# A decode kernel's last weight row in two halves, with a branch hint, a load and a copy moved

## The chip, the cores and the metric

The kernel runs on one core of one Trainium2 chip. The metric is the device time of one execution, in microseconds. Each timed run also gives the **span** of the profile, from the core's first counted instruction to its last; the execution time is about 1.25 us longer than the span in the kernel before.

## The reference, cut to what matters

One token goes through two blocks, whose results are added: attention over a cache of 65,536 positions (32 query heads on 4 cached heads), and a small network of layers with w1 to w4.

```python
xn = _layernorm(x)
return x + _A_ref(xn, k_cache, v_cache, wq, wo) + _B_ref(xn, w1, w2, w3, w4)
# _A_ref: q = xn @ wq; softmax(q k^T / sqrt(128)) v for each head; @ wo
# _B_ref: ... h2 = gelu(layernorm(x1) @ w3) @ w4;  w4 is 3584 x 1024
```

The caches are 134 MB, all inputs 170 MB, the output is 1024 numbers of two bytes. Every input is read once. So the kernel is a stream of loads with work beside it, and a short tail after the last byte.

## The kernel before

All large loads go through SyncE's queue into three slots of on-chip memory: wq, w1, w2, w3, then K and V blocks in turn, then wo, and last w4 in four transfers of 17, 7, 3 and 1 "rows". Such a row is what one step of the contraction needs: 1024 columns on each of 128 partitions, 2 KB a partition. TensorE's program runs the four cached heads in a loop; the instructions before and after the loop are straight code.

The tail, cut to what the change touches:

```python
w4_parts = [(0, 17), (17, 7), (24, 3), (27, 1)]
...
def out_rows(items, reads, last=False):          # [1,256] products in 4 column groups
    for lhs, rhs in items:
        for jj in range(4):
            ... e.matmul(S_ps[32*jj:32*jj+1, 0, 0:256], lhs, rhs[:, 256*jj:256*jj+256], ...)
...
def wo_rows():
    ...
    _op(q_dve, lambda e: e.tensor_copy(pT_f[0:1, 0, :], S_ps[0:1, 1, :]), ...)
    _op(q_act, lambda e: e.activation(pT_f[32:33, 0, :], S_ps[32:33, 1, :], ACTF.Copy), ...)
...
for i, (r0, nr) in enumerate(w4_parts):
    out_rows(...)                                # waits for transfer i
_op(q_dve, lambda e: e.tensor_copy(orow[:, :], OUT), ...)
ev_out = _dma(q_sp, chan("out"), lambda e: e.dma_start(out=out..., in_=orow[0:97:32, :]), ...)
```

The products of w4 start inside TensorE's tail, behind a hint. The hint belongs to a dummy branch at the end that is never taken, whose target is the tail itself:

```python
nc.br(name + "_b", engines=[e]);  label(name + "_b")
hint = eng.mark_branch_hint_location()           # the hint instruction stands here
q.emit(eng, q.ops[at:])                          # the products of w4
eng.br_eq(one, 1, on_true=name + "_end", on_false=name + "_t")
label(name + "_t");  eng.nop(nofuse=True)
eng.br_eq(one, 0, on_true=name + "_b", on_false=name + "_end").branch_hint(hint)
```

## Time and profile before

| | kernel before |
|---|---|
| execution time, median of 3 runs | 400.37 us |
| span of the profiled run | 399.0 us |
| VectorE busy, TensorE busy | 55%, 44% |
| bytes read from HBM, mean rate | 169.87 MB, 426 GB/s |
| last transfer of w4 lands | 396.47 us |

The busy lines of a page are averages over stages and say little here; the line of DMA slices, full from end to end, says nearly everything. The prediction shows it with the lines of the tail. Two more lines of the page, from its list of DMA queues (packets, MB, share of the 16 engines' time):

```profile
q8 instruction: 4, 0.07, 0.1%
q14 instruction: 3, 0.02, 0.0%
```

The page calls them "instruction": they are not data but the engines' own code, and it counts their time on the same 16 DMA engines. Inside the span stand four packets of 16 KB, 1.02 to 1.11 us each, and three of 8 KB, 0.32 us each.

### The profile page before, as it was taken

The page shows a single profiled execution, that of the slowest core. Times are in us where ns is not written, and L with a number is a line of the kernel's source. Part 1 is how long each engine was busy: PE and PEld are TensorE (multiplying, and loading weights), DVE is VectorE, ACT ScalarE, POOL GpSimd, SP SyncE. Part 2 cuts the span into 40 slices and gives each one's busy share as a digit, 9 for nine tenths or more (in the row PEclk, how much of TensorE's full clock was granted, in tenths as well). Part 3 has the DMA queues.
Part 4 walks back from the last instruction along what each step waited for, and adds up shares of the span by engine and source line. Part 5 has one row for each costly group of instructions (what it writes and reads, how often), then busy time and mean ns, then how long its engine had stood idle before and what let it go on. Part 6 is the DMA issues. An engine that isn't in the chain of part 4 may idle for free.

```text
span 399.0 us, 3448 instructions
## 1 busy us (share of the span) xinstructions
PE 176.1 (44%) x1539; PEld 58.8 (15%) x1484; DVE 221.3 (55%) x260; ACT 23.9 (6%) x50; POOL 7.6 (2%) x31
## 2 busy tenths in 40 slices
PE   0034768148034713570357036413651462147394
PEld 0011334012001200120012001101120110012232
DVE  0024221995298549843984597269647952896200
ACT  1000000011001100110011002001100110011000
POOL 5000000000000000000000000000000000000000
PEclk9998656556755765565557555855585558555979
DMA  9999899999999999999999999999999999999995
GB/s 421 421 386 494 383 428 480 447 416 427 421 420 435 420 466 453 421 427 421 420 440 420 453 460 427 421 421 420 434 434 440 473 427 421 420 421 427 431 410 233
DMA packets 3759, 169.97 MB, mean 426 GB/s; under 512 B 548, under 2 KB 552, under 8 KB 808
## 3 DMA queue, kind: packets, MB, share of 16 engines
q1 hardware_dynamic: 3608, 169.87, 98.8%
q8 instruction: 4, 0.07, 0.1%
q10 hardware_dynamic: 144, 0.00, 0.0%
q14 instruction: 3, 0.02, 0.0%
HBM read 169.87 MB, written 0.00 MB: 426 GB/s over the span
## 4 chain that ended last, share of the span: by engine, by line
DMA 58%; DVE 25%; PE 13%; issue 1%; ACT 1%; SPq 1%; POOL 0%
DMA KV<-in_A_k_cache_dram 45%; DVE KV L460 18%; DMA KV<-in_B_w_dram 8%; DMA KV<-in_A_x_dram 6%; PE S_ps L411 3%; PE OT_ps L518 2%; DVE mrow L481 2%; PE M_ps L426 2%; PE S_ps L474 2%; PE S_ps L379 2%; ACT p_sb L496 1%; DVE Yall L395 1%; DVE pT_f L509 1%; PE PT_ps L505 1%; DVE pT_f L419 1%
## 5 line engine op out<-in xcount | busy, mean ns | idle before, releaser
L460 DVE STREAM_TRANSPOSE KV<-KV 128x4096 f32<-128x4096 f32 x32 | 140.3, 4421 | 43.3 <-DMA KV<-in_A_k_cache_dram 43.3
L474 PE MATMUL S_ps<-KV,Ycur 128*32 128x512 bf16 x512 | 60.7, 623 | 127.2 <-DVE KV L460 127.2
L518 PE MATMUL OT_ps<-KV,pT_f 128*32 128x512 bf16 x512 | 46.2, 500 | 1.2 <-DVE pT_f L509 1.2
L474 PEld LDWEIGHTS S_ps<-KV,Ycur 128*32 128x32 bf16 x512 | 14.3, 126 | 159.0 <-DVE KV L460 141.4
L496 ACT ACTIVATE p_sb<-S_ps,brun 128x1024 bf16<-128x1024 f32 x16 | 17.8, 1113 | 275.0 <-DVE brun L494 174.5
L509 DVE STREAM_TRANSPOSE pT_f<-PT_ps 128x512 f32<-128x512 f32 x32 | 22.5, 702 | 14.0 <-PE PT_ps L505 14.0
L481 DVE TENSOR_REDUCE mrow<-S_ps 128x1 f32<-128x1024 f32 x16 | 19.3, 1206 | 11.3 <-PE S_ps L474 11.3
L484 PE MATMUL M_ps<-Rm,Lmat 128*128 128x16 bf16 x16 | 3.1, 194 | 38.1 <-DVE Rm L482 38.1
L505 PE MATMUL PT_ps<-p_sb,permR 128*128 128x512 bf16 x32 | 18.4, 576 | 0.8
L529 DVE SCALAR_TENSOR_TENSOR O_acc<-O_acc,ff,OT_ps 128x512 f32<-128x512 f32 x12 | 9.0, 748 | 13.9 <-PE OT_ps L518 13.9
L518 PEld LDWEIGHTS OT_ps<-KV,pT_f 128*32 128x32 bf16 x512 | 12.9, 114 | 23.6 <-issue 15.5
L411 PE MATMUL S_ps<-KV 128*32 128x512 bf16 x88 | 12.6, 565 | 2.7 <-DVE KV L359 2.7
L339 DVE CAST KV<-KV 128x8 f32<-128x8 bf16 x1 | 0.2, 171 | 22.1 <-DMA KV<-in_A_x_dram 22.1
L578 PE MATMUL S_ps<-KV,o_bf 128*1 128x512 bf16 x64 | 9.4, 466 | 5.0 <-DMA KV<-in_A_wo_dram 5.0
L426 PE MATMUL M_ps<-ident_f,pT_f 64*128 64x2 f32 (+2 forms) x32 | 7.9, 372 | 2.5 <-DVE pT_f L419 2.5
L484 PEld LDWEIGHTS M_ps<-Rm,Lmat 128*128 128x128 bf16 x16 | 1.7, 104 | 49.3 <-DVE Rm L482 49.3
L582 DVE COPY pT_f<-S_ps 1x512 f32<-1x512 f32 x1 | 0.7, 679 | 14.4 <-PE S_ps L578 14.4
L426 PEld LDWEIGHTS M_ps<-ident_f,pT_f 64*128 64x128 f32 (+2 forms) x32 | 7.7, 326 | 5.0 <-DVE pT_f L419 3.4
L419 DVE COPY pT_f<-S_ps 64x512 f32<-64x512 f32 (+1 forms) x3 | 2.1, 685 | 11.3 <-PE S_ps L411 11.3
L364 PE MATMUL M_ps<-KV 8*128 8x8 bf16 x1 | 0.2, 181 | 16.0 <-DVE Dmat_f L363 16.0
L505 PEld LDWEIGHTS PT_ps<-p_sb,permR 128*128 128x128 bf16 x32 | 3.3, 103 | 26.7 <-ACT p_sb L496 14.7
L379 PE MATMUL S_ps<-KV 128*32 128x512 bf16 x64 | 6.2, 571 | 1.4 <-DVE KV L359 1.4
(88 smaller groups left out, 85.6 us busy)
## 6 DMA issues: line engine op xcount, KB each, us to landing
KV<-in_B_w_dram SPq DMA_DIRECT2D x1, 7168.0 KB, 48.2
KV<-in_B_w_dram SPq DMA_DIRECT2D x1, 4352.0 KB, 27.4
KV<-in_B_w_dram SPq DMA_DIRECT2D x2, 2048.0 KB, 28.2
KV<-in_B_w_dram SPq DMA_DIRECT2D x1, 1792.0 KB, 31.4
KV<-in_B_w_dram SPq DMA_DIRECT2D x1, 768.0 KB, 32.7
KV<-in_B_w_dram SPq DMA_DIRECT2D x1, 256.0 KB, 32.9
KV<-in_A_k_cache_dram SPq DMA_DIRECT2D x8, 46.6
KV<-in_A_v_cache_dram SPq DMA_DIRECT2D x8, 27.9
```

What stands on the lines that cost most here:

```text
L379: fns.append(lambda e, j=j, b=b, jj=jj: e.matmul(S_ps[32 * jj:32 * jj + 32, b, :], xn_bf[:, j:j + 1].broadcast_to([P, 32]), KV[:, 0, j * H ...
L411: fns.append(lambda e, j=j, k=k, mv=mv: e.matmul(S_ps[32 * (k % 4):32 * (k % 4) + 32, bank + k // 4, :], vec[:, j:j + 1].broadcast_to([P, ...
L426: fns.append(lambda e, b=b, nb=nb, c=c: e.matmul(M_ps[:, c0 + 16 * b + c:c0 + 16 * b + 4 * nb:4], pT_f[0:32 * nb, b, c:512:4], ident_f[0:3 ...
L460: _op(q_dve, lambda e: e.transpose(out=KV32[:, s, o:o + 4096], in_=KV32[:, s, o:o + 4096]), reads=[b_KV[s][sub]], writes=[b_KV[s][sub]], l ...
L474: fns.append(lambda e, we=we, cm=cm, mv=mv: e.matmul(S_ps[32 * cm:32 * cm + 32, n % 4, :], Ycur[:, we, :, :].rearrange("p a g -> p (a g)") ...
L481: _op(q_dve, lambda e: e.reduce_max(mrow[:, k:k + 1], S_ps[:, 2 * k:2 * k + 2, :].rearrange("p b c -> p (b c)"), axis=AX.X), reads=b_S[2 * ...
L496: _op(q_act, lambda e: e.activation(p_sb[:, :, :].rearrange("p b c -> p (b c)"), S_ps[:, 2 * k:2 * k + 2, :].rearrange("p b c -> p (b c)") ...
L505: _op(q_pe, lambda e: e.matmul(PT_ps[:, :], permR[:, :], p_sb[:, n % 2, :], start=True, stop=True), reads=[b_p[n % 2], b_const], writes=[b ...
L509: _op(q_dve, lambda e: e.transpose(out=pT_f[:, n % 2, :], in_=PT_ps[:, :]), reads=[b_PT], writes=[b_pT[n % 2]], loop=True)
L518: fns.append(lambda e, q=q, q4=q4: e.matmul(OT_ps[32 * q4:32 * q4 + 32, g % 2, :], pT_bf[:, n % 2, q, :, 1], KV[:, s, 8192 * sub + 512 * q ...
L529: _op(q_dve, lambda e: e.scalar_tensor_tensor(out=O_acc[:, 0:512], in0=O_acc[:, 0:512], scalar=ff[:, k:k + 1], in1=OT_ps[:, k, :], op0=ALU ...
L578: _grp(q_pe, [lambda e, j=j, jj=jj: e.matmul(S_ps[32 * jj:32 * jj + 1, 1, :], o_bf[:, j:j + 1], KV[:, 0, j * D + 512 * jj:j * D + 512 * (j ...
```

## The change

The change wants a shorter tail. The last w4 row comes in two transfers of 512 columns. The first 24 rows are summed in one bank (of PSUM, the memory that TensorE writes its sums to) and copied to on-chip memory while the rest is under way; rows 24 to 26 are multiplied in 128-column pieces into one bank for each half; and each half of the output has its own last products, its own addition and its own store, the first from ScalarE, the second from SyncE. The second half reuses the weights that the first half has loaded. The order of the output's columns in the banks is changed to fit, in the products of wo too (not shown). Three small edits come with it: the tail's dummy branch goes, and the hint stands for the loop's own closing branch; x is loaded by SyncE, after wq, instead of by ScalarE; the second row of wo's sums is copied by VectorE.

```diff
-        _dma(q_act, chan("x"), ... x_bf ...)
         kv_load(0, "s0", rows_src(A_wq, 0, 8), 8 * HQD)
+        _dma(q_sp, chan("x"), ... x_bf ...)
...
-            _op(q_act, lambda e: e.activation(pT_f[32:33, 0, :], S_ps[32:33, 1, :], ACTF.Copy), ...)
+            _op(q_dve, lambda e: e.tensor_copy(pT_f[32:33, 0, :], S_ps[32:33, 1, :]), ...)
...
-        w4_parts = [(0, 17), (17, 7), (24, 3), (27, 1)]
+        w4_parts = [(0, 17 * D), (17 * D, 24 * D), (24 * D, 27 * D), (27 * D, 27 * D + 512), (27 * D + 512, 28 * D)]
...
-        for i, (r0, nr) in enumerate(w4_parts):
-            out_rows(...)
-        _op(q_dve, lambda e: e.tensor_copy(orow[:, :], OUT), ...)
-        ev_out = _dma(q_sp, chan("out"), ...)
+        for i in range(n_bulk):                   # n_bulk = 2
+            out_rows(i)
+        _op(q_dve, lambda e: e.tensor_copy(ost, S_ps[:, 0, 0:256]), ...)
+        for r in range(24, 27):
+            out_halves(r, (0, 1), 2, first=(r == 24))
+        for hf, q_out in ((0, q_act), (1, q_sp)):
+            out_halves(27, (hf,), 3 + hf, last=True)
+            _op(q_dve, lambda e, hf=hf: e.tensor_tensor(out=orow[:, 128*hf:128*hf+128], in0=ost[...], in1=S_ps[:, 2 + hf, 0:128], op=ALU.add), ...)
+            ev_out.append(_dma(q_out, chan("out%d" % hf), ... 512 outputs ...))
...
+        loop_br = [... the last branch of TensorE so far, which closes the loop ...][-1]
         q_pe.emit(nc.tensor, q_pe.ops[marks[-1]:pe_cut])
-        hinted_tail(nc.tensor, q_pe, pe_cut, "pe")
+        bass.BassInstruction(loop_br).branch_hint(nc.tensor.mark_branch_hint_location())
+        q_pe.emit(nc.tensor, q_pe.ops[pe_cut:])
```

## The prediction

> **What bounds the kernel now.** I read the page from the top: busy shares first, then the slices, then the chain, then the stretches in which the change lies. VectorE, the busiest engine, is busy for 55% of the span, TensorE for 44%. The slices show what is full:
>
> ```profile
> DMA  9999899999999999999999999999999999999995
> GB/s 421 421 386 494 383 428 480 447 416 427 421 420 435 420 466 453 421 427 421 420 440 420 453 460 427 421 421 420 434 434 440 473 427 421 420 421 427 431 410 233
> ...
> HBM read 169.87 MB, written 0.00 MB: 426 GB/s over the span
> ```
>
> The 16 DMA engines are busy from the first slice to the last, which falls to a half. 169.87 MB at about 430 GB/s are 395 us, so all but some 4 us of the 399.0 us are the transfer of inputs, and the change moves as many bytes. Time can only come out of the two ends, or be lost as a hole in the stream. I look for holes in SyncE's waits:
>
> ```profile
> SPq L290 <- PE OT_ps L518: 255.5, 7, 38.8
> ```
>
> SyncE waits to reuse the one V slot; this wait is long, but the page gives 27.9 us from issue to landing of a V load. One load is 8.39 MB, 19.5 us at 430 GB/s, so about 8 us of other transfers still lie ahead of it when it is issued. A delay of TensorE or VectorE under 8 us never reaches the end. The last stretch, from the timeline:
>
> ```profile
> 395.86 0.50 PE L566 MATMUL S_ps<-KV,gh_bf 128*1 128x256 bf16 x12 [0.92 <-DMA KV<-in_B_w_dram]
> ...
> 396.51 0.28 PE L566 MATMUL S_ps<-KV,gh_bf 128*1 128x256 bf16 x4 [0.16 <-DMA KV<-in_B_w_dram]
> 396.85 0.42 DVE L648 CAST orow<-S_ps 128x256 bf16<-128x256 f32 x1 [7.29 <-PE S_ps L566]
> 397.30 0.62 SPq L649 DMA_DIRECT2D out_dram<-orow  x1
> ```
>
> The last w4 row lands at 396.47. Then come its four products, the cast, the store's issue, and (SyncE's waits) 1.0 us until the store has landed. This exposed tail is 399.0 - 396.47 = 2.5 us, 0.6% of the span: the change's direct prize is a part of that.
>
> A second reading: the last row does not land at once. Windows of the last microseconds:
>
> ```profile
> 394.00:395.00 1.00, 0.93 (x28) 0.57 (x28) 0.00 (x0) 0.00 (x0) 0.00 (x0) 1.00 0.50 186
> 395.00:396.00 1.00, 0.14 (x8) 0.14 (x12) 0.00 (x0) 0.00 (x0) 0.00 (x0) 1.00 0.25 96
> ```
>
> The last two columns are the DMA share and GB/s: half the engines' time is used from 394 to 395, a quarter from 395 to 396. The trace's sixteen semaphore steps of the last row say why: eleven engines end it between 394.58 and 395.28, five between 396.03 and 396.47. The laggards were made earlier. The trace has four instruction packets of 16 KB, at 48.1, 84.3, 120.7 and 376.8, each of 1.02 to 1.11 us; after each, one more engine trails by about that much, and [...]it never catches up. So the last landing is late by about 1.2 us through instruction fetch.
>
> [...]x's 16-byte packets, on ScalarE's queue, alternate with wq's 64 KB packets, and x lands at 22.1, no sooner than wq (21.9).[...]
>
> **The change, part by part.**
>
> *x on SyncE.* Its 128 packets last 9 ns each, 8 to an engine, plus one semaphore write of 9: 0.08 us, now behind wq instead of between its packets. Equal DMA time, and x lands near 22.1 as before. Worth 0.
>
> *wo's rows copied by VectorE.* ScalarE's 0.59 us copy becomes a second VectorE copy of 0.68. The two start 0.72 apart as it is, so this phase ends about 0.1 later. But the first w4 products end at 392.80 and the next wait until 394.00 for data: 1.2 us of slack. Worth 0.
>
> *The branch hint.* The old tail had a hint and a dummy branch (a move of 29 ns, the hint of 40 ns); the new one has a hint only, for the loop's branch, at the same place. [...]I expect the same four packets and 0 from it.
>
> *The last row in halves.* What it costs: a 2 KB packet takes 84 ns, a 6 KB one 238, hence 7 ns fixed and 77 for the bytes. Eight 1 KB packets take 8 x 46 = 0.37 us, two halves 0.74 against 0.67, plus a semaphore write of 9 ns: the last landing moves from 396.47 to about 396.54. The first half lands at 396.17.
> What it saves: [...]The cast of 256 columns (0.42) becomes an addition of 128: 0.28, as the 128-column VectorE operations on PSUM at L362 and L546 took. That is 0.14 less. Sum: +0.07 - 0.05 - 0.14 = -0.12 us.
> What could hold it up: rows 24 to 26 now need 24 products, from 395.86. The old 12 took 0.50, of which 0.27 is the last one's own latency, so 21 ns apart; at that spacing 24 are issued by 396.36, the first half's four by 396.44, just ahead of the last landing. The first addition would run 396.70 to 396.98, and the second, due at 396.87, would wait 0.12. Narrower products may issue faster. The gain is therefore 0 to 0.12. The bulk sum's copy (0.42) is done by about 395.4, hidden. The first half's store, from ScalarE, is issued about 0.3 sooner than the second and runs beside it. The chain behind the last addition (0.03 + 0.62 + 1.0) stays as long, unless 256 B rows are slower.
>
> **Rivals.** (1) *The fetch pattern changes.* [...]one engine loses about 1.05 us around 388 to 392. On one of eleven punctual engines, it ends near 396.3, still behind the laggards: nothing. On one of five laggards, it ends near 397.5: +1.0 us. Conversely, if the early fetches were gone the landing would come 1.2 us sooner; the code before the loop is unchanged, which speaks against it. (2) *TensorE becomes the bound of the tail*: narrower products double the instructions[...]. The 21 ns spacing speaks against it. (3) *Small stores*:[...] (4) *The stream hides all*: the bytes and the laggards set the landing, and the halves give nothing: 400.4.
>
> **Range and chances.** The metric was 1.25 us over the span in the profiled run and should stay so. 400.37 - 0.12 gives 400.25 us. Rivals 2 and 3 push up by some tenths, rival 1 either way by about 1; most weight stays near zero: 399.7 to 400.8. Two per cent are 8.0 us, more than three times the whole tail; only a hole in the stream could lose so much, and none of the parts makes one. Faster by over 2%: 0.01; within 2%: 0.98; slower: 0.01.
>
> **What would show it.** The DMA slices stay at 9; the last landing of w4 is near 396.54, the one before near 396.2; VectorE's last operation is 0.28 long and starts near 396.87; four 16 KB instruction packets at about the old times. A fifth packet, other times of the four, or no laggards among the last row's semaphore steps would mean rival 1; a TensorE group ending over 0.35 us after the last landing rival 2; a final wait of SyncE over 1.1 us rival 3. The prediction fails if x, landing later, delays the early loads' issue by over 8 us, or if the fetch pattern shifts on many engines.

The sum came to -0.12 us; its -0.05, for shorter products, is an estimate from no trace, and the times 396.70 and 396.87 and the 400.25 us contain it. The trace of the kernel before shows: the worst engine ends 1.94 us behind the first in the load that lands at 69.5, and 2.00 in the one that lands at 359.95. The 0.27 us of a product of 256 columns is measured: 272 ns in the median, there.

## The result, and the profile after

| | before | after |
|---|---|---|
| median of the runs taken together, 6 each | 400.42 us | 400.69 us |
| lowest to highest | 400.35 to 400.58 | 400.53 to 401.30 |
| ratio of the runs | | 1.0009, interval 0.9996 to 1.0022 |
| span of the profiled run | 399.0 | 399.3 |
| execution time minus span, profiled run | 1.25 | 1.42 |

A ratio is the mean time of one kernel's runs over that of the other's of the same rounds, so it is not quite the ratio of the medians. The time lies in the predicted range. But the sign is not the predicted one: instead of 0.12 us less, 0.27 us more.

The stream is as full as it was. The page of the changed kernel:

```profile
DMA  9999999999999999999999999999999999999995
GB/s 420 420 384 490 388 428 479 440 422 420 427 427 427 427 473 440 427 420 427 427 428 427 466 440 427 420 421 433 427 433 466 440 427 420 420 433 427 418 418 225
...
HBM read 169.87 MB, written 0.00 MB: 425 GB/s over the span
```

So no hole was torn into it. The tail in the timeline (start, duration, engine, line, operation; in brackets the idle time before and what ended it):

```profile
396.26 0.45 PEld L593 LDWEIGHTS S_ps<-KV,gh_bf 128*1 128x1 bf16 x28 [1.25 <-DMA KV<-in_B_w_dram]
396.26 0.58 PE L593 MATMUL S_ps<-KV,gh_bf 128*1 128x128 bf16 x28 [0.95 <-DMA KV<-in_B_w_dram]
396.96 0.22 PE L562 MATMUL S_ps<-KV,gh_bf 128*1 128x128 bf16 x4
396.97 0.55 DVE L684 TENSOR_TENSOR orow<-pT_f,S_ps 128x128 bf16<-128x128 f32 x2 [1.18 <-PE S_ps L593]
397.29 1.10 ACTq L686 DMA_DIRECT2D out_dram<-orow  x1
397.54 0.62 SPq L686 DMA_DIRECT2D out_dram<-orow  x1
```

The last half lands at 396.92, by the semaphore steps of the trace. The reader is to see two things. First, the tail behind the landing works as intended: from 396.92 to the last store's issue at 397.54 are 0.62 us, where the kernel before needed 397.30 - 396.47 = 0.83. Second, the landing itself is 0.45 us later than before, of which only 0.07 had been expected. And the profiled execution has 0.17 us more outside the span than before. Both have to be explained. Here is a clue to the second, the queue lists of the changed kernel, first of the page (the span), then of a window from 398 to 401 us:

```profile
q8 instruction: 5, 0.08, 0.1%
q14 instruction: 2, 0.02, 0.0%
```

```profile
DMA packets 17, 0.01 MB, mean 3 GB/s; under 512 B 16, under 2 KB 16, under 8 KB 16
...
q14 instruction: 1, 0.01, 0.8%
```

TensorE's 16 KB packets are five instead of four: the new one is at 394.38. (That they are TensorE's shows in the run with the hint alone, below: only TensorE's program differs there, and a 16 KB packet comes at 393.52 and another moves from 120.7 to 197.9.) And one of the 8 KB packets is missing from the span: it stands at 399.87, after SyncE's last wait is over (399.26). In the kernel before, that third one was at 393.65.

### The profile page after: what moved, and what is told of

It reads as the page before. It is cut to its first block, busy times and chain, and to the rows that moved or that the text cites. A ratio compares the mean times of both kernels' runs of the same rounds, so it can differ in the third digit from the quotient of the medians.

```text
span 399.3 us, 3479 instructions
## 1 busy us (share of the span) xinstructions
PE 177.2 (44%) x1555; PEld 59.5 (15%) x1496; DVE 222.6 (56%) x263; ACT 23.3 (6%) x49; POOL 7.6 (2%) x31
## 4 chain that ended last, share of the span: by engine, by line
DMA 58%; DVE 25%; PE 13%; issue 1%; ACT 1%; SPq 0%; POOL 0%; DVEq 0%
DMA KV<-in_A_k_cache_dram 45%; DVE KV L460 17%; DMA KV<-in_B_w_dram 8%; DMA KV<-in_A_x_dram 5%; PE S_ps L411 3%; PE OT_ps L518 3%; DVE mrow L481 2%; PE M_ps L426 2%; PE S_ps L474 2%; PE S_ps L379 1%; ACT p_sb L496 1%; DVE Yall L395 1%; PE PT_ps L505 1%; DVE pT_f L509 1%; DVE pT_f L419 1%
## 5 line engine op out<-in xcount | busy, mean ns | idle before, releaser
L518 PE MATMUL OT_ps<-KV,pT_f 128*32 128x512 bf16 x512 | 47.6, 516 | 0.8 <-DVE pT_f L509 0.8
L411 PE MATMUL S_ps<-KV 128*32 128x512 bf16 x88 | 12.1, 536 | 2.7 <-DVE KV L359 2.7
```

Of the source, the lines that this page charges most:

```text
L411: fns.append(lambda e, j=j, k=k, mv=mv: e.matmul(S_ps[32 * (k % 4):32 * (k % 4) + 32, bank + k // 4, :], vec[:, j:j + 1].broadcast_to([P, ...
L518: fns.append(lambda e, q=q, q4=q4: e.matmul(OT_ps[32 * q4:32 * q4 + 32, g % 2, :], pT_bf[:, n % 2, q, :, 1], KV[:, s, 8192 * sub + 512 * q ...
```

## The experiments

Every run has its own span and execution time, so each kernel can be split into span and remainder. The spans are given to 0.1 us a run. Means over all timed runs; the kernel before was run 27 times in the company of these kernels:

| kernel | runs | time | span | time minus span |
|---|---|---|---|---|
| before | 27 | 400.49 | 399.23 | 1.26 |
| changed (three times) | 16 | 400.69 | 399.25 | 1.44 |
| halves only | 5 | 400.49 | 399.14 | 1.35 |
| hint only | 5 | 400.51 | 399.20 | 1.31 |
| x on SyncE only | 5 | 400.55 | 399.28 | 1.27 |
| changed, old hint | 5 | 400.46 | 399.02 | 1.44 |
| changed, no hint (twice) | 10 | 400.36 | 399.10 | 1.26 |
| changed, old hint, one store | 5 | 400.28 | 399.02 | 1.26 |
| changed, no hint, one store | 5 | 400.52 | 399.26 | 1.26 |
| two banks, one store | 5 | 400.92 | 399.64 | 1.28 |
| no-operations on VectorE | 4 | 400.47 | 399.18 | 1.29 |

The scatter of single runs is 0.07 to 0.32 us (standard deviation), so a mean of five stands to about 0.1. What follows rests on means of many runs and on durations inside the traces, which repeat to a few hundredths.

### The halves alone

The changed kernel with its three small edits undone: the old tail with dummy branch, x and the second copy on ScalarE again.

```diff
-        bass.BassInstruction(loop_br).branch_hint(nc.tensor.mark_branch_hint_location())
-        q_pe.emit(nc.tensor, q_pe.ops[pe_cut:])
+        hinted_tail(nc.tensor, q_pe, pe_cut, "pe")
-        _dma(q_sp, chan("x"), ...)      # after wq
+        _dma(q_act, chan("x"), ...)     # ahead of it
-            _op(q_dve, lambda e: e.tensor_copy(pT_f[32:33, 0, :], ...))
+            _op(q_act, lambda e: e.activation(pT_f[32:33, 0, :], ...))
```

> The kernel before with the halved last row alone (own products, sums, two stores); the old hint, x on ScalarE and wo's copy on ScalarE kept. Theory A (the loss comes from instruction fetch that the new hint lets through, the halves work as predicted): median 400.2 to 400.35, about 0.1 to 0.2 under the kernel before; four 16 KB instruction packets; chain from the last landing to the last VectorE end about 0.60 us. Theory B (the halves cost more than they save: smaller packets, two stores): 400.6 to 400.8, as the full change.

Measured: median 400.50, ratio 1.0000 (0.9986 to 1.0013): outside both ranges, between them. The parts are clearer. From the last landing (396.96) to the last store's issue (397.58) it takes 0.62 us; only four 16 KB packets are there; and the 8 KB packet stands after the span, at 399.79. So the halves win what they should inside the tail, the small packets cost only a little, and something is given back later. Both theories were incomplete.

### The hint alone

The kernel before with the hint exchanged.

```diff
-        hinted_tail(nc.tensor, q_pe, pe_cut, "pe")
+        bass.BassInstruction(loop_br).branch_hint(nc.tensor.mark_branch_hint_location())
+        q_pe.emit(nc.tensor, q_pe.ops[pe_cut:])
```

> The kernel before with only the hint exchanged (hint for the loop's back edge, no dummy branch). Theory A: 400.6 to 400.9 with a wider spread between runs than the kernel before, and a fifth 16 KB instruction packet in the last 10 us. Theory B: 400.4, no fifth packet, same spread as before.

Measured: median 400.39, ratio 1.0002 (0.9988 to 1.0016). The median is below theory A's range; the spread, 400.31 to 400.92, is about that of the kernel before in this company (400.30 to 400.84). The fifth packet is there, at 393.52. It costs nothing: the last row lands at 396.45, against 396.47 before. So theory A was right about the packet and wrong about its price. Another packet moved too: the third 16 KB packet came at 197.9, in the loop's second round, instead of 120.7, in its first, at the same place of the code. All traces with the new hint show this (197.9 to 200.3), none without it (120.4 to 123.1). Its delay ends on one engine either way: behind it one more of the sixteen trails the first by over 1.2 us, three instead of two in the kernel before, four instead of three in the first profile of the changed kernel.

### The changed kernel with the old hint

> The changed kernel with the old hint and dummy branch back in its place. Theory A: 400.2 to 400.4, narrow spread, no 16 KB packet after 380 us. Theory B: 400.6 to 400.8. Theory C (x on SyncE is what disturbs): 400.6 to 400.8 too, but then halves_only is at 400.3.

```diff
-        bass.BassInstruction(loop_br).branch_hint(...)
+        hinted_tail(nc.tensor, q_pe, pe_cut, "pe")
```

Measured: median 400.47, ratio 0.9999 (0.9986 to 1.0013), a narrow spread, 400.36 to 400.54, slightly above theory A's range and below the others'. No 16 KB packet after 380, as expected. The span is 0.21 us under the kernel before's mean; the remainder is 1.44. That is the whole puzzle in one row of the table: **the gain is in the span, and it is lost after the span.**

### The changed kernel again

> The changed kernel as it is, for its spread and a second profile in this company. All theories: 400.5 to 401.2. Theory A: again five 16 KB instruction packets, one of them after 390 us; the laggards of the last row sit elsewhere than in the first profile if the fetch times vary from run to run.

Measured: median 400.63, ratio 1.0003 (0.9990 to 1.0017). Again five packets of 16 KB, the late one at 393.79. Its engine can be seen in the semaphore steps: up to rows 24 to 26 eleven engines are punctual and five late, from the first half on ten and six; the six end the last half between 396.19 and 396.85, and the worst of them was the worst before the packet came. So the packet hit a punctual engine, and the end is set elsewhere.

This profile shows another loss. Windows of its tail, and below of the first profile of the changed kernel (columns after the stretch and its length: busy time of TensorE, weight loads, VectorE, ScalarE, GpSimd, then the granted share of TensorE's clock, DMA share, GB/s):

```profile
396.20:397.00 0.80, 0.80 (x32) 0.61 (x28) 0.00 (x0) 0.00 (x0) 0.00 (x0) 0.52 0.01 4
397.00:397.80 0.80, 0.21 (x8) 0.00 (x0) 0.48 (x2) 0.00 (x0) 0.00 (x0) 0.50 0.00 0
```

```profile
396.20:397.00 0.80, 0.62 (x32) 0.41 (x28) 0.03 (x1) 0.00 (x0) 0.00 (x0) 1.00 0.02 8
397.00:397.80 0.80, 0.18 (x4) 0.00 (x0) 0.52 (x2) 0.00 (x0) 0.00 (x0) 1.00 0.00 0
```

The clock is 0.52 and 0.50 in the first and 1.00 in the second. In all traces TensorE's clock is granted in full for 13.65 us from somewhere between 382.1 and 385.4 (384.18 before, 385.19 in the first profile of the changed kernel), and then falls to a half, between 395.8 and 399.1 (397.83 and 398.84); the time differs from one execution of the same kernel to the next, and no trace shows why. Where it falls before the last products, the 128-column product takes 312 ns instead of 216, and the way from the last landing to the last store's issue takes 0.89 us here instead of 0.62. The kernel before pays for the same thing only 0.93 instead of 0.83 (in the profiles of the runs with the hint alone and with the no-operations). So the halved tail, with its many narrow products right behind the landing, gains 0.21 us when the clock is full and 0.04 to 0.14 when it is not; this was so in 2 of the 9 profiles of halved kernels.

### No-operations on VectorE

The kernel before, with 128 no-operations put into VectorE's stream inside the loop, to make its code longer by what the author took for one 8 KB packet (an estimate: before the first three 16 KB packets the trace of the kernel before counts 190, 439 and 707 matmuls and weight loads of TensorE, so 249 and 268 to a packet).

```diff
+            if m == 1:
+                for _ in range(128):
+                    q_dve.op(lambda e: e.nop(nofuse=True), tick=False)
             issue(6 + 2 * m)
```

> The kernel before with 128 no-operations[...] in VectorE's stream, placed in the loop where VectorE has idle time. Theory A (the end is set by the DMA engine that also carries instruction fetch; the two 8 KB packets of the traces are VectorE's code, on one engine, 0.98 us each): a third 8 KB packet inside the stream, the worst laggard about 1.0 us further back, 401.1 to 401.5. Rival (laggards are harmless, or 8 KB packets belong to another engine): 400.3 to 400.6.

Measured: median 400.47, ratio 0.9999, and no further packet. But the trace lists 271 records on VectorE, as before, and none of them is a no-operation. Whether they were executed unseen or dropped on the way to the chip, the run doesn't say; so it tells nothing of whose code the 8 KB packets are. A void experiment, not a refutation.

### The changed kernel without a hint

```diff
-        bass.BassInstruction(loop_br).branch_hint(nc.tensor.mark_branch_hint_location())
```

> The changed kernel without any hint. Theory A1 (the new hint does not hold back the fetch of the next block): same as the changed kernel, 400.6 to 400.9, a 16 KB packet near 394. Theory A2 (the new hint itself causes the late packet): no 16 KB packet after 380, and 400.4 to 400.5.

Measured the first time: median 400.32, below both ranges, ratio 0.9993 (0.9979 to 1.0007). The late 16 KB packet is there without any hint, at 394.18. With the old hint it is absent in six of seven profiles (it came once, in the kernel with two banks below, whose tail has more instructions). So in these profiles the packet stayed away with the old hint, but for that one, and came with the new one and, here, with none. It cost nothing where that could be read: with the hint alone the last row landed at 396.45, against 396.47. Unexpected was the rest: no 8 KB packet after the span, and a remainder of 1.26 us, although ScalarE issues its store as in the changed kernel and ends as late, at 398.23.

### x alone

```diff
-        _dma(q_act, chan("x"), ...)
         kv_load(0, "s0", rows_src(A_wq, 0, 8), 8 * HQD)
+        _dma(q_sp, chan("x"), ...)
```

> The kernel before with x loaded by SyncE only. As predicted: 400.35 to 400.55, same as the kernel before; x lands about 22.1 us. Rival (a second queue at the start changes how the engines start, and with it which engine trails): 400.6 or more, worst laggard over 2.2 us behind the first.

Measured: median 400.55, ratio 1.0001 (0.9988 to 1.0015). Same, as predicted. The worst engine trails the first by 2.17 us at 358, inside the range of the other kernels (2.00 to 2.51).

### Two banks, one store

An attempt at a better tail: the kernel before with all its w4 products in two banks of 128 columns, copied at the same time by VectorE and ScalarE, the last row in one transfer, one store.

```diff
-                        S_ps[32*jj:32*jj+1, 0, 0:256], lhs, rhs[:, 256*jj:256*jj+256],
+                        S_ps[32*jj:32*jj+1, 2*hf, 0:128], lhs, rhs[:, 256*jj+128*hf:256*jj+128*hf+128],   # hf = 0, 1
...
-        _op(q_dve, lambda e: e.tensor_copy(orow[:, :], OUT), ...)
+        _op(q_dve, lambda e: e.tensor_copy(orow[:, 0:128], S_ps[:, 0, 0:128]), ...)
+        _op(q_act, lambda e: e.activation(orow[:, 128:256], S_ps[:, 2, 0:128], ACTF.Copy), ...)
```

> The kernel before with the output sums in two PSUM banks of 128 columns, copied by VectorE and ScalarE at the same time, one store; w4's last row in one transfer, old hint, x as before. The last landing to the store's issue should take about 0.66 us instead of 0.81, and the last row keeps its 2 KB packets: 400.2 to 400.35. Rival (224 narrow products make TensorE late, more so when its clock is halved in the tail): 400.5 or more.

Measured: median 400.87, ratio 1.0009 (0.9995 to 1.0023), but in every one of its five runs above the median of the kernel before. In the profile the clock fell to a half at 396.37 and the products were late, as the rival had it: 0.88 us from landing to issue. But there is a second loss, and it is the instructive one. The store is issued at 397.59, and SyncE then waits 1.5 us for it instead of 1.0:

```profile
SPq L73 <- DMA out_dram<-orow: 1.5, 1, 1.5
```

At 398.56, in the middle of this wait, an 8 KB packet of code runs for 0.46 us; the last of the store's four data packets starts when it is over, at 399.01, and is the last to be complete, 0.4 us after the others. ScalarE had ended its copy at 397.48.

### One store, and ScalarE out of the tail

This pointed to the missing piece. Here are the end of ScalarE's last recorded instruction and the start of the third 8 KB packet, in all traces so far that have one:

| kernel | ScalarE ends | third 8 KB packet |
|---|---|---|
| before; hint only; x only; no-operations | 390.18; 389.19; 390.42; 389.20 | 393.65; 392.42; 393.72; 392.65 |
| two banks | 397.48 | 398.56 |
| halves only; changed, old hint | 398.41; 398.18 | 399.79; 399.72 |
| changed (three profiles) | 398.39; 398.65; 398.04 | 399.87; 400.09; 399.48 |

The packet follows ScalarE by 3.2 to 3.5 us while w4 is still being loaded, and by 1.1 to 1.5 when all of it has landed. So I formed a new theory: ScalarE's stream fetches one more 8 KB packet after its last instruction (whose code the packet holds, no view says; it is argued from these times); in the kernel before this happens beside the loads and costs nothing, and the change, by giving ScalarE a store that is issued until 398.4, moves it behind the end. The test takes away ScalarE's store and nothing else: one store from SyncE, after both additions, beside the old hint, so that it is compared with the changed kernel with the old hint.

```diff
-            ev_out.append(_dma(q_out, chan("out%d" % hf), ... 512 outputs of half hf ...))
+        ev_out = [_dma(q_sp, chan("out"), ... both halves, 4 x 2 x 128 ..., reads=b_orow)]
```

> The changed kernel with the old hint and one store, issued by SyncE after both halves are summed, so that ScalarE has nothing to do in the tail. Theory D (the halves do win about 0.2 us of span, and lose it after the span: ScalarE, busy until 398.4 with its store, fetches its last 8 KB of code at about 399.8 instead of inside the stream): execution time minus span back from 1.44 to about 1.27 us, no instruction packet after 399, span 399.0 to 399.1 as with two stores; 400.2 to 400.35. Rival (the extra time after the span belongs to the halves' code or to TensorE's hint): 1.44 us stays, 400.45.

Measured: median 400.29, ratio 0.9995 (0.9981 to 1.0008). The remainder is 1.26, as in the kernel before; the span 399.02, as with two stores. ScalarE ends at 366.07, and its packet is at 369.7, inside the stream; the page counts three 8 KB packets in the span again:

```profile
q8 instruction: 4, 0.07, 0.1%
q14 instruction: 3, 0.02, 0.0%
```

The tail of this kernel:

```profile
396.77 0.22 PE L562 MATMUL S_ps<-KV,gh_bf 128*1 128x128 bf16 x4
396.78 0.55 DVE L683 TENSOR_TENSOR orow<-pT_f,S_ps 128x128 bf16<-128x128 f32 x2 [1.18 <-PE S_ps L593]
397.35 0.67 SPq L685 DMA_DIRECT2D out_dram<-orow  x1
```

From the landing at 396.73 to the issue are 0.62 us again, although one store waits for both halves: the second addition was the last thing before SyncE's store in the changed kernel too. The first half's early store won nothing. This is the fastest kernel in the mean, 400.28 +/- 0.05 against 400.49 +/- 0.03 for the kernel before (standard errors), a gain of about 0.2 us or 0.05%; its own interval still includes "same". Five runs don't establish this: the changed kernel without a hint had a mean of 400.26 in its first five runs and 400.45 in the next five.

### One store, no hint

> The same with no hint at all. Theory D: as one_store, 400.15 to 400.35, with a late 16 KB packet near 394 that costs nothing. Rival (the single store takes from the span what it gives after it): 400.4 or more.

```diff
-        hinted_tail(nc.tensor, q_pe, pe_cut, "pe")
+        q_pe.emit(nc.tensor, q_pe.ops[pe_cut:])
```

Measured: median 400.37, ratio 1.0000 (0.9987 to 1.0014), one run at 401.04; the median is just above the range expected. The remainder is 1.26 as expected, but no 8 KB packet follows ScalarE's end (366.39) at all: the third packet is missing, as in the other kernel without a hint. From 360 us to past the end, the instruction packets of this kernel, and below of the one with the old hint:

```profile
q8 instruction: 2, 0.03, 0.3%
```

```profile
q8 instruction: 1, 0.02, 0.2%
q14 instruction: 1, 0.01, 0.0%
```

So this run can't test where ScalarE's packet falls. The profiled run, at 400.63, shows where its time went: the last half lands at 397.03, the latest of all the profiles, and the tail behind it is the usual 0.62. In this trace the worst engine is 2.52 us behind the first from 264 us on; in the kernel before's it was 1.98. How such a distance comes about is told in the next section.

### The changed kernel without a hint, and as it is, once more

> The changed kernel without a hint, once more, beside the changed kernel: does its 400.3 hold, with 1.26 us after the span and no packet after 399 in the trace, although ScalarE issues a store as in the changed kernel? If the hint matters: 400.2 to 400.35 again. If the first was chance: 400.5 to 400.8.

> The changed kernel a third time, in the same company: 400.6 to 400.8, 1.40 to 1.55 us after the span, an 8 KB packet after 399, a 16 KB packet near 394.

Measured, without a hint: median 400.48, ratio 0.9999 (0.9985 to 1.0012), above the range that I had set. But the remainder is 1.25 again, in all of its five runs between 1.22 and 1.28, and again there is no third 8 KB packet, though ScalarE ends at 398.39. Measured, as changed: median 400.51, below the range that I had set, ratio 1.0004 (0.9990 to 1.0017), remainder 1.42, the packet at 399.48. So of the first pair's difference the part in the remainder, 0.18 us, came back, and the part in the span mostly did not.

These two kernels are the control that the theory lacked. ScalarE's store and its late end are the same in both; what differs, along with the remainder, is the packet. So it is not the late store itself that lengthens the remainder; nor is it the hint itself, for the one-store kernel has one and a remainder of 1.26. Over all profiles: the third 8 KB packet is there in the eleven of kernels with a branch hint, old or new, and in none of the three without one.

## Why the prediction was right or wrong

**What was right.** The bound: the stream stayed full, and nothing in the change moved the time by even 0.1%. The 0.98 for "within 2%" came from the size of the exposed tail, 2.5 us against 8 us, and that needed no more than two lines of the profile. x on SyncE and the second copy on VectorE: worth 0 as said; the two copies took 1.40 us from the first's start to the second's end, with ScalarE 1.31, and the next stage waited for data anyway. The halves, term by term:

| term | predicted | measured |
|---|---|---|
| later landing by small packets | +0.07 | +0.05: rows 24-26 to the end took 0.69 to 0.71, before 0.64 to 0.66 |
| shorter products (-0.05) and sum | -0.19 | -0.21: landing to issue 0.62 (seven profiles at full clock), before 0.83; a product 216 ns against 272, the last addition 0.29 against 0.42 for the cast |
| second addition held up | 0 to 0.12 | 0 at full clock; the narrow products issued in time: 28 in 0.58 us, 0.22 of it the last one's own, so 13 ns apart against 21 |
| store | 0 | +0.03: 1.06 against 1.03; its 256 B packets took 18 to 24 ns, those of 512 B 29 to 39 |
| sum | -0.12 | about -0.13 at full clock |

The mean span of all 46 runs of halved kernels with two or one store is 399.16 +/- 0.03, that of the kernel before 399.23 +/- 0.03: the direction agrees, but 0.07 +/- 0.05 is too coarse to confirm the size. That rests on the durations in the table.

**What was wrong: "The metric was 1.25 us over the span in the profiled run and should stay so."** This is the step that failed. It became 1.44 in 16 runs of the changed kernel. The working had asked of each added instruction what it costs in the span, and not what its engine does afterwards. ScalarE's store takes 1.10 us to issue, so its stream ends at 398.4 instead of 390.2, and the 8 KB packet that comes after it, once beside w4 (393.65), comes after the end (399.87). Taking ScalarE out of the tail brought the 1.26 back and left the span as it was; so did leaving ScalarE's store and having no hint, with which the packet does not come. With +0.18 for this term, -0.12 becomes +0.06. The means of the table differ by +0.20; the other 0.14 is in the span, and is the difference that stays open below. That the time fell into the predicted range is owed to its width.

**Wrong without effect: the hint.** "I expect the same four packets" did not hold; there are five, as rival 1 had said they might be. Its estimate of the price held: on a punctual engine the packet ends (395.49 in the first profile of the changed kernel) before the laggards do (396.23 to 396.92).

**Mis-sized: what a fetch costs an engine.** The text set the delay at the packet's own 1.05 us, and counted four packets for five laggards. The fifth is the engine that the first two 8 KB packets had, at 55 and 259 us. The data packet behind a fetch is stretched as well: in the traces the 64 KB packet after a 16 KB fetch takes 2.88 to 2.97 us instead of 2.42, after each of the first two 8 KB fetches 3.08. So a fetch costs its engine about 1.5 us (1.05 and the 0.5 of the stretching) and 0.98 us (0.32 and 0.66), estimates from these times. In the traces one lag grows by 0.96 to 0.99 at the second 8 KB packet (from 1.35 to 2.33 in the first profile of the changed kernel); with what the first one gave it, this is the engine that lands last or among the last. How far back it starts differs between executions by some tenths, and that is most of the difference between the last landings of the profiles, 396.45 to 397.03. The 0.45 us by which the first profile of the changed kernel landed later is therefore 0.05 from the halves and the rest from this; a single pair of profiles must not be read more finely than that.

**What stays open.** With the rest of the kernel unchanged, the runs with the new hint have a span of 399.25 +/- 0.06, those without a hint 399.10 +/- 0.05. On its own, the new hint changed nothing (399.20 against 399.23). No trace shows a mechanism for the 0.15, and it may be scatter: with one store the sign is the other way (without a hint 399.26 +/- 0.15, with the old one 399.02 +/- 0.04). Why the third 8 KB packet comes only in kernels with a hint in TensorE's program, no run explains; in the one-store kernel it comes 21 us before TensorE reaches its hint (369.68 and 391.20), so the hint's execution doesn't cause it. The packet's price isn't the same everywhere either: the halves alone have it after the end too, at 399.79, and a remainder of 1.35, in their five runs between 1.30 and 1.40. And whose code the 8 KB packets are, the first two above all, stays open.

## What to carry to other kernels

Ask of an engine that is given work in the tail not only how long the work takes but what the engine would otherwise have done by then: here the 8 KB code fetch that came after ScalarE's last instruction was hidden as long as ScalarE finished early (packet at 393.65, 1.26 us after the span), and not when it finished at 398.4 (packet at 399.87, 1.44 us). When execution time and span are both given, subtract them for every run; a gain in the one can be lost in the other, and neither alone shows it. And where a saturated stream sets the end, look at each DMA engine's own landing: here the slowest landed at 396.47 and the eleventh of sixteen at 395.28, and code fetches that the page puts at 0.1% of the engines' time had decided which it was.
